# Causal convolution and two-layer MLP on one core: taps' diagonals from a bf16 table, a first convolution in 21 places, the first half of w_in in two pieces around x

## The chip, the cores and the metric

The kernel runs on one NeuronCore of a Trainium2 chip. A core has TensorE (matrix products into PSUM), VectorE, ScalarE and GpSimd (elementwise work; GpSimd also issues loads), SyncE (issues transfers) and they share 16 DMA engines. Each engine works through its own instructions in order; they wait for each other through semaphores. The metric is the device time of one execution in microseconds. Before the change it is 681.5 us, the median of 4 runs from 681.38 to 681.66.

## The reference

x has shape [8, 4096, 192], weight [8, 7], w_in [192, 2048], w_out [2048, 192], all in float32.

```python
w = softmax(weight)                       # over the 7 taps of each of 8 heads
y[b, s, c] = sum_k w[c // 24, k] * x[b, s + k - 6, c]     # zero before the start
h = y @ w_in                              # [32768, 2048]
out = maximum(0.01 * h, h) @ w_out        # [32768, 192]
```

The two products make up nearly all of the arithmetic; the convolution is a sum of seven shifted and scaled copies of x.

## The kernel before

**Layout.** Two batch rows are worked on together. The 192 channels are three chunks of 64; partitions 0 to 63 hold a chunk of the one row, 64 to 127 the same chunk of the other. xt is x in this layout (channels on partitions, time along the free dimension), yt the convolved x, g the activated first layer. A block is 512 time steps of a pair of rows; there are 32. The first two blocks are each done as two halves of 256 columns (groups 0 to 3), the others whole (groups 4 to 33).

**The main loop.** For each group, `mm1` forms the first layer in steps: step u makes 512 columns' worth of PSUM for both rows (`ph`, two buffers), in products of one 64-channel chunk with 128 columns of w_in (L494). ScalarE applies the leaky ReLU from PSUM into g (L501). Between the steps stand slots of the second layer for the group before (L511 for the first groups, L574 later). Meanwhile VectorE convolves the next group, tap by tap (L226, L232), GpSimd loads x three blocks ahead (L99), and SyncE transposes it by DMA (L117) and stores the results. The order on each engine is written out by hand; a plan tells how many second-layer slots follow each step.

**The beginning.** Group 0 has nothing ahead of it, so its convolution is done by TensorE. The softmaxed taps are split into bf16 parts (high, middle, low). `select` spreads them over the partitions by a product with a 0/1 matrix `sel`; VectorE copies the high and middle parts from PSUM to `whm` in float32 (L407). A diagonal of 64x64 for each tap, chunk and part is the 64-wide identity `ident2` times the tap: VectorE makes seven at once (`diag_wide`, L413), ScalarE makes some singly (`diag_each`, L421). `pe_conv_jobs` returns a list of jobs for one chunk: for each part and tap, two products of a 64x64 diagonal with the shifted xt, one per row (L257). TensorE works in four tiles of 64x64, so two chunks can run side by side if one of them writes crosswise (`cross=True`: row 0 to partitions 64 to 127 and the other way round); `apart` gives its two rows a PSUM buffer each. `run` interleaves lists. In group 0 the order is: chunk 0's first part alone; its second part beside chunk 2's first; chunk 1's one part beside chunk 2's second; chunk 1's other part alone. `evac` scales by 1/sum (`rsum`) and writes yt (L271, L276 on VectorE, L452 on ScalarE).

Behind it, TensorE transposes the next quarter of x (`transpose_first(1)`, from `x_rows`, L188), VectorE copies it to xt (`evac_first`, L199), and `mm1` of group 0 begins. Group 1's convolution is split: chunk 1 by VectorE, chunks 0 and 2 by TensorE in cuts between the first-layer steps of group 0 (`CUTS`: after steps 1, 3 and 5). The transposes of the third quarter stand after step 6, their copies at the end of the group.

**w_in.** It is loaded by GpSimd in two halves (`load_w_in`, L314), rows 0 to 127 and 128 to 191 each. Both tile rows need all chunks on their own partitions, so VectorE copies chunks across: `spread_down` (L320) and `spread_up` (L323). The order of loads on GpSimd's queue is: w_in's first half, x_rows 1, w_in's second half, x_rows 2, w_out in two, x_half 3 in six, then x_bf for block 2 on. VectorE spreads the second half between taps of group 1.

**Buffers.** `psum_o` (tag po) has four banks in turn, for the transposes, the convolution's sums and the second layer; `psum_h` (tag ph) two buffers of two banks, first used by the warm-up products (`warm`) and by `wps`, the selected taps.

## Time and profile before

| what | value |
|---|---|
| median of 4 runs | 681.5 us |
| the profiled execution | 681.55 us |
| its span, first to last instruction | 679.8 us |
| TensorE products, busy | 675.6 us, 99% |
| VectorE, busy | 481.2 us, 71% |
| ScalarE, busy | 518.7 us, 76% |
| granted TensorE clock, mean | 1.00 |
| first matmul of the first layer | 9.58 us |
| first matmul of the second layer | 17.83 us |

The span is what the trace covers; 1.75 us of the execution lie around it. A row of the timeline or of a group of instructions names the line, the engine, the operation, output<-input with their shapes, and how often it stands there; times are in us from the span's start, the mean of one instruction in ns. In brackets stands how long the engine was idle before it, and what ended that. The chain of waits is followed back from the last instruction: at each step to what released it. [...]

### The profile page before, as it was taken

Reading aid. Unit: us, or ns where it says so; the run is one execution under the profiler, and the core shown is the slowest. Engines: PE = TensorE matmul, PEld = TensorE weight load, DVE = VectorE, ACT = ScalarE, POOL = GpSimd, SP = SyncE. Lnnn points to the kernel's source line nnn. Section 1 sums busy time; section 2 is a strip of 40 time slices with the busy share of each in tenths; the row PEclk is TensorE's granted clock in tenths of the full one; section 3 lists DMA queues with packets and bytes.
Section 4 is the critical chain, followed back from the end, with each engine's and each line's share of the span. In section 5 each row is a group of like instructions: output and inputs, shape, how many; then the busy total and the mean of one; then the engine's idle time right before and its main releaser. Section 6 shows DMA issues by size and latency. Waiting matters only on the chain.

```text
span 679.8 us, 27093 instructions
## 1 busy us (share of the span) xinstructions
PE 675.6 (99%) x12444; PEld 446.9 (66%) x12444; DVE 481.2 (71%) x811; ACT 518.7 (76%) x608; POOL 146.3 (22%) x205
## 2 busy tenths in 40 slices
PE   9999999999999999999999999999999999999998
PEld 6997666666666666666666666666666666666667
DVE  7989468766768667778667687667786676876612
ACT  7899777777877778777777877777777777777781
POOL 7455220222210222211222012222022220000000
PEclk9999999999999999999999999999999999999999
DMA  9998864666556557456556475566465573321123
GB/s 152 92 114 106 59 87 80 80 62 75 88 85 89 69 56 90 81 87 87 61 68 89 79 95 71 59 85 93 74 87 67 62 96 71 72 56 32 35 49 94
DMA packets 213890, 53.27 MB, mean 78 GB/s; under 512 B 209296, under 2 KB 213392, under 8 KB 213776
## 3 DMA queue, kind: packets, MB, share of 16 engines
q0 software_dynamic: 98752, 13.97, 30.2%
q1 hardware_dynamic: 115008, 37.57, 28.0%
q8 instruction: 97, 1.59, 1.0%
q14 instruction: 17, 0.14, 0.1%
q10 hardware_dynamic: 16, 0.00, 0.0%
HBM read 28.31 MB, written 25.17 MB: 79 GB/s over the span
## 4 chain that ended last, share of the span: by engine, by line
PE 98%; DMA 1%; POOL 0%; issue 0%; DVE 0%; POOLq 0%
PE ph L494 49%; PE acc L574 44%; PE po L511 5%; DMA x_rows<-in_x_dram 1%; PE acc L257 0%; POOL w_in L314 0%; PE ptr L188 0%; POOL x_rows L148 0%; POOL sel L300 0%; DVE o_sb L624 0%; POOL ident masks.py:199 0%; POOL sel L298 0%; POOL ident masks.py:197 0%; POOLq masks.py:199 0%; POOLq L736 0%
## 5 line engine op out<-in xcount | busy, mean ns | idle before, releaser
L501 ACT ACTIVATE g<-ph 128x1024 bf16<-128x1024 f32 x512 | 496.6, 1021 | 140.8 <-PE ph L494 140.6
L232 DVE SCALAR_TENSOR_TENSOR yt<-xt,wk,yt 128x512 bf16<-128x512 bf16 (+1 forms) x582 | 381.6, 730 | 0.2
L494 PE MATMUL ph<-yt,w_in 64*64 64x512 bf16 (+2 forms) x6048 | 377.1, 369 | 0.0
L574 PE MATMUL acc<-g,w_out 64*64 64x512 bf16 x5568 | 339.9, 376 | 0.0
L494 PEld LDWEIGHTS <-w_in 64*64 64x64 bf16 (+1 forms) x6048 | 229.3, 131 | 103.0 <-issue 0.8
L574 PEld LDWEIGHTS <-w_out 64*64 64x64 bf16 x5568 | 178.4, 118 | 118.8
L99 POOL DMA_DIRECT2D x_bf<-in_x_dram x180 | 133.9, 773 | 409.6 <-DMA xt<-x_bf 407.5
L596 DVE STREAM_TRANSPOSE o_t<-acc 128x512 f32<-128x512 f32 x87 | 73.3, 884 | 181.7 <-PE acc L574 181.7
L511 PE MATMUL po<-w_out,g 64*128 64x192 bf16 (+1 forms) x640 | 36.8, 243 | 0.0
L511 PEld LDWEIGHTS <-g 64*128 64x128 bf16 (+1 forms) x640 | 32.6, 95 | 3.2 <-issue 0.4
L226 DVE TENSOR_SCALAR yt<-xt,wk 128x512 bf16<-128x512 bf16 (+1 forms) x97 | 29.7, 335 | 2.9 <-DMA xt<-x_bf 2.8
L584 ACT COPY junk<-junk 128x1 f32<-128x1 f32 x58 | 11.1, 192 | 4.1
L624 DVE COPY o_sb<-po 128x192 f32<-128x192 f32 x8 | 2.8, 356 | 6.8 <-PE po L511 4.1
L257 PE MATMUL acc<-xt,diag 64*64 64x256 bf16 x140 | 5.5, 272 | 0.2 <-ACT xt L199 0.2
L624 ACT COPY o_sb<-po 128x192 f32<-128x192 f32 x16 | 5.1, 323 | 0.3
L257 PEld LDWEIGHTS <-diag 64*64 64x64 bf16 x140 | 4.3, 106 | 1.3 <-issue 0.6
L358 PE MATMUL warm<-const-bfloat16-1.0 128*128 128x512 bf16 (+3 forms) x12 | 3.9, 478 | 0.8 <-PEq L736 0.8
L152 POOL DMA_DIRECT2D x_half<-in_x_dram x6 | 4.2, 718 | 0.8 <-DMA w_in<-in_moe_w_in_dram 0.8
L358 PEld LDWEIGHTS <-const-bfloat16-1.0 128*128 128x128 bf16 x12 | 1.4, 132 | 2.5 <-issue 2.5
L148 POOL DMA_DIRECT2D x_rows<-in_x_dram x4 | 2.9, 742 | 0.0
L413 DVE TENSOR_TENSOR diag<-ident,whm 128x448 bf16<-128x448 bf16 (+1 forms) x5 | 2.6, 580 | 0.0
L421 ACT ACTIVATE diag<-ident,whm 128x64 bf16<-128x64 bf16 x10 | 2.5, 338 | 0.0
(47 smaller groups left out, 23.7 us busy)
## 6 DMA issues: line engine op xcount, KB each, us to landing
out_dram<-o_t SPq DMA_DIRECT2D x112, 192.0 KB, 4.6
x_bf<-in_x_dram POOLq DMA_DIRECT2D x180, 64.0 KB, 3.3
out_dram<-o_sb SPq DMA_DIRECT2D x8, 192.0 KB, 3.2
xt<-x_bf SPq DMA_TRANSPOSE x90, 3.8
w_out<-in_moe_w_out_dram POOLq DMA_DIRECT2D x2, 384.0 KB, 7.8
out_dram<-o_t SPq DMA_DIRECT2D x8, 96.0 KB, 2.2
out_dram<-o_sb SPq DMA_DIRECT2D x8, 96.0 KB, 1.7
w_in<-in_moe_w_in_dram POOLq DMA_DIRECT2D x2, 256.0 KB, 5.4
```

Source lines behind the costliest of these rows:

```text
L99: ins = nc.gpsimd.dma_start(out=t[:, c, :, e, :], in_=src[2 * rp + e, :, :, c * CH : (c + 1) * CH],)
L226: lambda s=src, d=dst, c=c: nc.vector.tensor_scalar_mul(d, s, wk[:, c, 0:1])
L232: lambda s=src, d=dst, c=c, k=k: nc.vector.scalar_tensor_tensor(out=d, in0=s, scalar=wk[:, c, k : k + 1], in1=d, op0=mybir.AluOpType.mult, ...
L257: lambda k=k, p=p, a=a, ps=ps, to=to, acc=accs[e * apart]: nc.tensor.matmul(out=acc[to, :T], lhsT=diag[c][ps, p, k, :], rhs=xt[0][ps, c, a ...
L358: nc.tensor.matmul(out=wa[:, 0, 0:cols], lhsT=ones[:, 0:128], rhs=ones[:, 0:cols], start=True, stop=True,)
L494: nc.tensor.matmul(out=ph[m : m + M, e, i * T : (i + 1) * T], lhsT=w_in_of(f, e, c, m, m + M), rhs=y[ps, c, t0 : t0 + T], start=(c == chun ...
L501: act = nc.scalar.activation(out=g[blk][:, nf * u : nf * (u + 1), :, t0 : t0 + T], in_=ph.rearrange("p e (i t) -> p i e t", i=nf), func=my ...
L511: return nc.tensor.matmul(out=po[m], lhsT=g[b][ps, fc, e, s * 128 : (s + 1) * 128], rhs=w_out[ps, fc, :], start=start, stop=stop,)
L574: ins = nc.tensor.matmul(out=acc2[gi, r][e * CH : (e + 1) * CH, 0:T], lhsT=w_out_of(ps, fc, r), rhs=g[b][ps, fc, e, t0 : t0 + T], start=fi ...
L584: seal = nc.scalar.copy(out=junk, in_=junk)
L596: nc.vector.transpose(out=osb[gi, 0][:, 0 : T // GB, :, r], in_=acc2.pop((gi, r))[:, 0:T].rearrange("p (j k) -> p j k", k=GB),)
L624: ins = copy(out=o_sb[:, n % 2, :], in_=po.pop(n))
```

## The change

- `diag_wide` multiplies bf16 by bf16. The table `taps` holds each tap twice, side by side, in bf16, so that the innermost dimension of each operand is a pair of adjacent elements; it replaces `whm`. VectorE makes all six groups of seven diagonals, `diag_each` and ScalarE's ten are gone. The order on VectorE is new: chunk 0 and chunk 1 first, the small sums between, chunk 2 last.
- Group 0's convolution: chunks 0 and 1 run side by side in 14 places, then chunk 2 alone, in the new `pe_conv_quads`: each row's 256 columns are cut into two halves, one straight and one crosswise, so that all four tiles work, on 128 columns each. Its crosswise halves go to the two banks of `wps`. In all 14 places of 256 columns and 14 of 128, that is 21 places of 256 for the 28 before.
- One more warm-up product of 192 columns stands ahead of it.
- w_in comes in three pieces: 512, 512 and 1024 columns (`PIECES`). The first piece is loaded before x_rows 1, the second and the third after it. The spreads of the second and third stand between the first taps of group 1.
- The first step of group 0 runs over the chunks outermost (`wide`), so that chunk 1 and chunk 2 are needed later in it. The order of chunks is 0, 1, 2.
- wk is formed before the last evacuation of group 0 instead of after the copies of x.
- Group 1's cuts are 6, 6 and 2 jobs instead of 6, 5 and 3; chunk 2 of it has its rows in two buffers (`apart`) and its second row is evacuated by ScalarE. The transposes of the third quarter and their copies now stand after step 5, ahead of the last cut.

```diff
--- before.py
+++ after.py
@@ -44,16 +44,13 @@
     NBLK = (B // 2) * NB
     NHALF = 2
     RUN = 4
-    NPEC = 3
     FILL = 48
-    VK = 4
-    FIRST = (0, 2, 1)
     SKEW = [(c, k) for k in range(2) for c in range(2)]
     pair = iter([(0, 2), (1, 2), (0, 3), (1, 3), (0, 4), (1, 4), (0, 5)])
     for k in range(K):
         SKEW += [(2, k), next(pair)]
     SKEW += [(1, 5), (0, 6), (1, 6)]
-    CUTS = {1: (0, 6), 3: (6, 11), 5: (11, 14)}
+    CUTS = {1: (0, 6), 3: (6, 12), 5: (12, 14)}
     GB = 32
     NR = D // (2 * GB)
 
@@ -277,6 +274,42 @@
 
         return jobs, evac
 
+    def pe_conv_quads(grp, c, crossed):
+
+
+        blk, t0, T = grp
+        n = T // 2
+        acc = psum_o.tile([128, ST], FP32, name="acc", tag="po")
+        accs = [(acc, acc), (crossed[:, 0], crossed[:, 1])]
+        jobs = []
+        for p in range(2):
+            for k in range(K):
+                a = BASE + k + blk * ST + t0
+                four = []
+                for h in range(2):
+                    for e in range(2):
+                        ps = slice(e * CH, (e + 1) * CH)
+                        to = slice((e ^ h) * CH, ((e ^ h) + 1) * CH)
+                        four.append(
+                            lambda k=k, p=p, a=a + h * n, ps=ps, to=to, acc=accs[h][e]: nc.tensor.matmul(
+                                out=acc[to, :n], lhsT=diag[c][ps, p, k, :],
+                                rhs=xt[0][ps, c, a : a + n],
+                                start=(k == 0 and p == 0),
+                                stop=(k == K - 1 and p == 1),
+                            )
+                        )
+                jobs.append(four)
+
+        def evac(straight, *scale):
+            y = yt[blk][:, c, t0 : t0 + T]
+            straight(y[:, 0:n], acc[:, :n], rsum[:, c, :])
+            for e in range(2):
+                ps = slice(e * CH, (e + 1) * CH)
+                frm = slice((1 - e) * CH, (2 - e) * CH)
+                scale[e](y[ps, n:T], crossed[frm, e, :n], rsum[frm, c, :])
+
+        return jobs, evac
+
     def run(*lists):
         for slots in zip_longest(*lists, fillvalue=()):
             for both in slots:
@@ -305,15 +338,18 @@
     nc.vector.tensor_copy(out=sel[:, :, 1, :], in_=sel[:, :, 0, :])
 
 
-    NPW = 2
-    WF = F // NPW
-    w_in = [const_pool.tile([128, NCH, WF], BF16, name=f"w_in{n}") for n in range(NPW)]
+    PIECES = [(0, RUN), (RUN, 2 * RUN), (2 * RUN, NFC)]
+    w_in = [
+        const_pool.tile([128, NCH, (b - a) * 128], BF16, name=f"w_in{n}")
+        for n, (a, b) in enumerate(PIECES)
+    ]
 
     def load_w_in(n, rows):
         ps, slot = ((0, 128), 0) if rows == 0 else ((0, CH), 2)
+        a, b = PIECES[n]
         nc.gpsimd.dma_start(
             out=w_in[n][ps[0] : ps[1], slot],
-            in_=moe_w_in[rows : rows + ps[1], n * WF : (n + 1) * WF],
+            in_=moe_w_in[rows : rows + ps[1], a * 128 : b * 128],
         )
 
     def spread_down(n):
@@ -323,7 +359,8 @@
         nc.vector.tensor_copy(out=w_in[n][CH:128, 1:3, :], in_=w_in[n][0:CH, 0:3:2, :])
 
     def w_in_of(f, e, c, m0, m1):
-        n, f = divmod(f, NFC // NPW)
+        n = min(f // RUN, len(PIECES) - 1)
+        f -= PIECES[n][0]
         slot = c if c == 2 else c ^ e
         a = f // RUN * RUN * 128 + f % RUN
         return w_in[n][
@@ -335,8 +372,9 @@
     make_identity(nc, ident)
     load_w_in(0, 128)
     load_first(1)
-    for rows in (0, 128):
-        load_w_in(1, rows)
+    for n in range(1, len(PIECES)):
+        for rows in (0, 128):
+            load_w_in(n, rows)
     load_first(2)
 
 
@@ -403,48 +441,45 @@
     cast_first(0, 0, nc.scalar.copy)
     cast_first(0, 1, nc.scalar.copy, slice(0, 1))
     cast_first(0, 1, nc.vector.tensor_copy, slice(1, 2))
-    whm = const_pool.tile([128, NCH, 2, K + 1], FP32, name="whm")
-    nc.vector.tensor_copy(out=whm, in_=wps_hm)
-
-
-    diag = [const_pool.tile([128, 2, K, CH], BF16, name=f"diag{c}") for c in range(NPEC)]
-
-    def diag_wide(c, p, n):
+    taps = const_pool.tile([128, NCH, 2, K + 1, 2], BF16, name="taps")
+    nc.vector.tensor_copy(
+        out=taps, in_=wps_hm[..., None].to_broadcast([128, NCH, 2, K + 1, 2])
+    )
+
+
+    diag = [const_pool.tile([128, 2, K, CH], BF16, name=f"diag{c}") for c in range(NCH)]
+
+    def diag_wide(c, p):
+
+
+        shape = [128, K, CH // 2, 2]
         nc.vector.tensor_mul(
-            diag[c][:, p, 0:n],
-            ident2[:, None, :].to_broadcast([128, n, CH]),
-            whm[:, c, p, 0:n, None].to_broadcast([128, n, CH]),
-        )
-
-    def diag_each(c, p, ks):
-        for k in ks:
-            nc.scalar.activation(
-                out=diag[c][:, p, k, :], in_=ident2,
-                func=mybir.ActivationFunctionType.Copy, scale=whm[:, c, p, k : k + 1],
-            )
-
+            diag[c][:, p].rearrange("p k (m t) -> p k m t", t=2),
+            ident2.rearrange("p (m t) -> p m t", t=2)[:, None].to_broadcast(shape),
+            taps[:, c, p, 0:K, None, :].to_broadcast(shape),
+        )
 
     warm(1, 192)
     transpose_first(0, lambda: select(wps_l, slice(2, 3)))
     wps_l = wps_l[:, :, 0, 0]
     warm(1, ST)
     warm(1, 384)
+    warm(1, 192)
     evac_first(0, nc.scalar.copy, nc.scalar.copy)
-    for p in range(2):
-        diag_wide(0, p, K)
-    diag_wide(2, 0, K)
-    diag_wide(1, 1, VK)
-    diag_wide(2, 1, K)
-    diag_each(1, 1, range(VK, K))
-    diag_each(1, 0, range(K))
     wml = const_pool.tile([128, NCH, K + 1], FP32, name="wml")
-    nc.vector.tensor_add(wml, wps_l, whm[:, :, 1])
     rsum = const_pool.tile([128, NCH, 1], FP32)
+    diag_wide(0, 0)
+    diag_wide(1, 0)
+    diag_wide(0, 1)
+    nc.vector.tensor_add(wml, wps_l, taps[:, :, 1, :, 0])
+    diag_wide(1, 1)
     nc.vector.scalar_tensor_tensor(
-        out=rsum, in0=wml[:, :, K:], scalar=1e-9, in1=whm[:, :, 0, K:],
+        out=rsum, in0=wml[:, :, K:], scalar=1e-9, in1=taps[:, :, 0, K:, 0],
         op0=mybir.AluOpType.add, op1=mybir.AluOpType.add,
     )
+    diag_wide(2, 0)
     nc.vector.reciprocal(rsum, rsum)
+    diag_wide(2, 1)
     spread_down(0)
     spread_up(0)
 
@@ -454,20 +489,18 @@
         )
 
     pe_0, evac_0 = pe_conv_jobs(groups[0], 0)
-    pe_2, evac_2 = pe_conv_jobs(groups[0], 2, cross=True, apart=True)
-    pe_1, evac_1 = pe_conv_jobs(groups[0], 1, (1, 0))
-    run(pe_0[:K])
-    run(pe_0[K:], pe_2[:K])
+    pe_1, evac_1 = pe_conv_jobs(groups[0], 1, cross=True, apart=True)
+    pe_2, evac_2 = pe_conv_quads(groups[0], 2, wps)
+    run(pe_0, pe_1)
     evac_0(act_scale)
-    run(pe_1[:K], pe_2[K:])
-    run(pe_1[K:])
-    evac_2(act_scale, nc.vector.tensor_scalar_mul)
-    evac_1(act_scale)
+    evac_1(nc.vector.tensor_scalar_mul, act_scale)
+    wk = const_pool.tile([128, NCH, K], FP32, name="wk")
+    nc.vector.tensor_add(wk, taps[:, :, 0, 0:K, 0], wml[:, :, 0:K])
+    nc.vector.tensor_mul(wk, wk, rsum.to_broadcast([128, NCH, K]))
+    run(pe_2)
+    evac_2(nc.vector.tensor_scalar_mul, act_scale, act_scale)
     transpose_first(1)
     evac_first(1, nc.vector.tensor_copy, nc.vector.tensor_copy)
-    wk = const_pool.tile([128, NCH, K], FP32, name="wk")
-    nc.vector.tensor_add(wk, whm[:, :, 0, 0:K], wml[:, :, 0:K])
-    nc.vector.tensor_mul(wk, wk, rsum.to_broadcast([128, NCH, K]))
 
 
     g, po, acc2, osb, seal = {}, {}, {}, {}, None
@@ -484,9 +517,14 @@
         y = yt[blk]
         nf = ST // T
         ph = psum_h.tile([128, 2, ST], FP32, name="ph", tag="ph")
-        chunks = range(NCH) if blk or t0 else FIRST
-        for n in range(nf * NCH):
-            i, c = n // NCH, chunks[n % NCH]
+        chunks = range(NCH)
+
+
+        wide = not (blk or t0 or u)
+        order = [(i, c) for i in range(nf) for c in chunks]
+        if wide:
+            order = [(i, c) for c in chunks for i in range(nf)]
+        for i, c in order:
             f = nf * u + i
             for e in range(2):
                 ps = slice(e * CH, (e + 1) * CH)
@@ -495,8 +533,9 @@
                         out=ph[m : m + M, e, i * T : (i + 1) * T],
                         lhsT=w_in_of(f, e, c, m, m + M),
                         rhs=y[ps, c, t0 : t0 + T],
-                        start=(c == chunks[0]),
+                        start=(c == chunks[0] and not (wide and i)),
                         stop=(c == chunks[-1]),
+                        skip_group_check=wide,
                     )
         act = nc.scalar.activation(
             out=g[blk][:, nf * u : nf * (u + 1), :, t0 : t0 + T],
@@ -672,22 +711,24 @@
                 mm1(grp, u, 128 if i <= NSW else CH)
                 if i == 0 and u == 0:
                     conv_1 = conv_jobs(groups[1], (1,))
-                    for job in conv_1[:3]:
-                        job()
-                    spread_down(1)
-                    spread_up(1)
-                    for job in conv_1[3:]:
+                    for n in range(1, len(PIECES)):
+                        conv_1.pop(0)()
+                        spread_down(n)
+                        conv_1.pop(0)()
+                        spread_up(n)
+                    for job in conv_1:
                         job()
                     pe_0, evac_0 = pe_conv_jobs(groups[1], 0)
-                    pe_2, evac_2 = pe_conv_jobs(groups[1], 2, cross=True)
+                    pe_2, evac_2 = pe_conv_jobs(groups[1], 2, cross=True, apart=True)
+                if i == 0 and u == 5:
+                    transpose_first(2)
+                    evac_first(2, nc.vector.tensor_copy, nc.vector.tensor_copy)
                 if i == 0 and u in CUTS:
                     cut = slice(*CUTS[u])
                     run(pe_0[cut], pe_2[cut])
                 if i == 0 and u == 5:
                     evac_0(nc.vector.tensor_scalar_mul)
-                    evac_2(nc.vector.tensor_scalar_mul, nc.vector.tensor_scalar_mul)
-                if i == 0 and u == 6:
-                    transpose_first(2)
+                    evac_2(nc.vector.tensor_scalar_mul, act_scale)
             jobs = ahead[per * j : per * (j + 1)]
             if T == ST:
 
@@ -697,8 +738,6 @@
                     job()
                 jobs = []
             mm2_slots(i, quota[j] - sum(early))
-            if i == 0 and j == 3:
-                evac_first(2, nc.vector.tensor_copy, nc.vector.tensor_copy)
             if i == 1 and j == 1:
                 load_x(3, transpose_x(2))
             for job in jobs:
```

## The prediction

> **What bounds the kernel now.** I read the page first, then the chain of waits, then the chain and the timeline of the first 22 us, where the whole change lies. The page:
>
> ```profile
> PE 675.6 (99%) x12444; PEld 446.9 (66%) x12444; DVE 481.2 (71%) x811; ACT 518.7 (76%) x608; POOL 146.3 (22%) x205
> PE 98%; DMA 1%; POOL 0%; issue 0%; DVE 0%; POOLq 0%
> ```
>
> TensorE is the bound: 99% busy, 98% of the chain. What is won before its steady work starts moves everything after it; nothing else can be won. The chain in order of time (start, length, what):
>
> ```profile
> 4.31 4.77 DMA x_rows<-in_x_dram
> ...
> 9.13 0.52 PE ptr L188 x11
> 9.65 1.43 PE ph L494 x24
> 11.08 0.78 PE acc L257 x24
> ...
> 15.53 0.46 PE acc L257 x12
> 15.98 0.78 PE ph L494 x12
> 16.76 0.46 PE ptr L188 x12
> 17.22 0.78 PE ph L494 x12
> 18.00 0.25 PE po L511 x6
> ```
>
> The first layer waits for the second x_rows load, landed at 9.08; from 9.13 on TensorE hardly stops. The timeline (start, span, engine, instructions, idle before):
>
> ```profile
> 4.44 2.57 DVE L413 TENSOR_TENSOR diag<-ident,whm 128x448 bf16<-128x448 bf16 x5
> 5.33 3.35 PE L257 MATMUL acc<-xt,diag 64*64 64x256 bf16 x84 [0.19 <-ACT xt L199]
> 9.69 0.62 DVE L199 COPY xt<-ptr 128x384 bf16<-128x384 bf16 x2 [0.51 <-PE ptr L188]
> 12.08 0.42 DVE L320 COPY w_in<-w_in 64x1024 bf16<-64x1024 bf16 x1
> 12.54 0.69 DVE L323 COPY w_in<-w_in 64x2048 bf16<-64x2048 bf16 x1
> 14.80 3.03 ACT L501 ACTIVATE g<-ph 128x1024 bf16<-128x1024 f32 x3 [0.17 <-PE ph L494]
> ```
>
> The first conv runs 5.33 to 8.68. It ends 0.45 before x_rows is there, so a shorter conv alone would win nothing.
>
> [...] 448 elements with an fp32 table take 618 ns, 256 take 418, thus 1.04 ns per element and 151 fixed. [...] four 64*64 matmuls start within 0.02 us, one such step per 0.11 us, and each change of shape costs about 0.09. [...]
>
> **The change, part by part.** One profiled execution: 681.55 us, span 679.8, 1.75 around it; the median is 681.5.
>
> *Diagonals.* Table copy of 96 instead of 48 elements: 0.20 to 0.25. Six products of 448 elements[...]: half of 467 ns, plus the fixed 151, is 384 ns each. Starts today lie 0.54 apart (467 + 70, as the next one overlaps the end of the last), so then 0.30. The small ops between (wml, rsum, reciprocal) fill 0.1 each. They start at 4.49, 4.79, 5.10, 5.49, 5.87, 6.26; the last ends at 6.65. The conv can start at 5.33 as now (it waits for ScalarE's xt; the extra warm-up matmul ends before). It needs the second pair of products at 6.10 (ready 5.88), the last two at 6.87 and 7.25 (6.26, 6.65). ScalarE's ten diagonals (2.5 us) go; they were hidden.
>
> *First conv.* Today: 28 steps x 0.11 = 3.1 us. Then: 14 full steps of four 256-column matmuls, 1.54, and 14 of 128 columns. The nearest row for these is L188, pairs of 128 columns with 64-column weights: 0.056 per pair. Bounds: 0.056 (14 x 0.056 = 0.78) and 0.11 (no gain from narrow columns, 1.54). I take 0.056. Last start 7.59.
>
> *x_rows.* Ahead of it stand 384 KB of w_in now, 192 KB then (counted as written, in bf16). The landings today are w_in0 6.6 and 8.1, x_rows 8.6 and 9.1, w_in1 11.0 and 11.6: the 704 KB after the first took 5.0 us, 140 KB/us. 192 KB less is 1.4 us, so about 7.7. The other limit is the issue: 4.31 plus the 3.3 us that x_bf takes when the queues are free is 7.6[...]. Transposes are due at 7.59 + 0.15 = 7.74. I count no wait; each 0.1 later costs 0.1.
>
> *First layer.* Transposes 0.30, change 0.15: it starts at 8.19 (9.58 now). Its new order needs chunk 1 at 8.43, chunk 2 at 8.65. The last full conv step starts at 6.76 and ends 0.27 later. Chunks 0 and 1 then leave by rows L452 and L276 (0.47 each): ScalarE 7.07 to 7.55 and 7.45 to 7.91, VectorE 7.33 to 7.80. VectorE comes there from the spreads of w_in0: a copy takes 0.42 for 1024 elements and 0.69 for 2048, thus 0.29 for 512, and the two at half size end at 7.30. Chunk 2: VectorE after the two wk instructions, 7.97 to 8.32 (0.35 for 128 columns: 0.48 less 0.13); ScalarE twice 0.37 from 7.85, done 8.48. Ready with 0.15 to spare. So far **-1.39**.
>
> *VectorE's next chain.* Two x copies from 8.33 (after the transposes) to 8.95, scale 9.06 to 9.35, then spread, tap, spread, tap: 0.29, 0.49, 0.42, 0.49 with 0.03 between; w_in1 is spread at 10.64. TensorE wants it after two first-layer steps (9.58 to 11.01 today, 1.43) and six conv steps (11.01 to 11.80, 0.79), at 8.19 + 1.43 + 0.79 = 10.41: a new stall of **+0.27**. Then 0.42, 0.49, 0.69: w_in2 at 12.86; TensorE arrives at 10.68 + 1.43 + 0.79 = 12.90 (six conv steps in this cut, five now, 0.11). So the fifth first-layer step starts at 12.90 against 13.91: **-1.01**. The loads: w_in2 is whole after the same 960 KB as w_in1 today (11.0 and 11.6); wanted at 11.2 and 12.2. If the first is 0.2 late, so is all after.
>
> *Transposes of x_rows2 moved up.* One change of shape less (-0.09), a 0.08 wait for ScalarE and one conv step (0.11) less, and x_rows2 landed at 13.0, before 14.3. But they stood between the group's seventh and eighth step. The next group's first step needs the buffer of the group's seventh step (there are two ph buffers): from that step's start it is, as today, 0.89 until its activation starts, 1.02 until it ends and 0.04 for the signal, thus 1.95. TensorE has 0.68 + 0.65 (two steps) + 0.25 (three second-layer slots) = 1.58 to do: stall **+0.37**. From the fifth step to the second group: 4.17 both times, so nothing is won. The added ScalarE evacuation (0.37 net) ends just when the seventh step is ready. Behind the stall stand only TensorE's own steps; w_out landed at 14.7 and 16.7, the second half is wanted at 18.8.
>
> *GpSimd's queue.* Two more issues of about 0.58: x_rows2, w_out and the first x_half issues come 1.1 later, but still well ahead of their data (w_out issued 7.5, landed 14.7). The later issues wait for landings that do not move. SP's transposes of x_half start at 17.13, after that landing; the group that reads the last at 27.1 would read it at 25.2 and it lands at 25.1: covered, with nothing to spare, but that conv has 4 us before TensorE needs it.
>
> *After.* VectorE is full from 18 to 46 us (28.16 of 28.2), but reaches group 2's conv some 2 us earlier, TensorE 1.0. From 65 on TensorE alone decides. Sum: -1.39 + 0.27 + 0.11 = **-1.01**; 681.55 - 1.0 = **680.5**.
>
> **The rivals.** *Narrow steps at 0.11.* Eight instructions per 56 ns is twice the densest the trace shows (four in L188)[...]. All shifts by 0.76: 681.3. For 0.056: the second set of loads follows the first after 0.03.
> *Single-rate products.* If the engine doesn't double over the broadcast pair, six products at 0.54 end at 8.0. Conv starts at 5.69 and stalls 0.4 in it, VectorE's spreads and evacuations follow, w_in2 is spread at 14.3, and the fifth step is 0.45 later than now: 682.0, slower. It decides from 0.46 us between products on. Against it: the 64-element add.
> *Loads late.* w_in in 1024-byte rows and two more completions could push x_rows past 7.74 or w_in2 past 11.2; with 0.5 late, 681.0.
> *No stalls.* If VectorE's chain runs 0.3 quicker than I sum: 680.2.
>
> **How the numbers follow.** Mine 0.64 (680.3 to 680.8), narrow steps in full or part 0.14, single rate 0.08, late loads 0.09, no stalls 0.05. The range, 680.1 to 681.5, leaves out single rate and the tails. 0.2% is 1.36 us, about what a measurement of this kernel can tell from no change; only a gain with no stall at all, or single rate with a further wait, passes it: faster 0.08, same 0.87, slower 0.05.
>
> **What would show it.** Products 0.38 us long; L254 and L294 together ending near 7.8; the first layer at 8.2 without a wait on x_rows; two TensorE gaps, about 0.3 before the third first-layer step (on L359) and 0.4 before the second group (on ScalarE). The prediction is wrong if the narrow steps lie 0.11 apart, products last 0.6, or x_rows lands after 7.8.

## The result

The kernel after takes 682.44 us (median of 41 runs, 681.47 to 683.23), the kernel before, measured beside it, 681.42 (61 runs, 681.05 to 682.54): a ratio of 1.0014, interval 1.0009 to 1.0018. So it is 1.0 us slower where 1.0 us faster was predicted, outside the range of 680.1 to 681.5; in size it lies within the 0.2% that the prediction calls about what a measurement can tell from no change, though the interval leaves out 1. The profiled execution of after took 682.56 us, its span is 680.9.

The page of the kernel after, busy time by engine and the chain of waits by engine:

```profile
PE 676.1 (99%) x12473; PEld 443.6 (65%) x12473; DVE 481.1 (71%) x814; ACT 517.0 (76%) x600; POOL 147.6 (22%) x207
PE 98%; DVE 1%; ACT 1%; issue 0%; DVEq 0%
```

TensorE's share is what it was. What changed is the remaining 2%: DMA is gone from the chain, VectorE and ScalarE have come in. The chain of after in order of time (start, length, what) says where:

```profile
5.87 0.18 DVE wml L474
...
7.44 0.75 DVE w_in L359
...
9.18 0.35 DVE yt L305
9.53 0.54 DVE xt L196 x2
...
10.17 0.65 DVE yt L223
...
11.69 0.43 DVE w_in L359
12.12 0.05 issue
12.17 1.50 PE ph L532 x23
13.66 0.78 PE acc L254 x24
14.45 1.03 PE ph L532 x12
15.48 0.02 issue
15.50 1.94 ACT g L540 x2
17.44 0.03 issue
17.47 0.47 ACT yt L487
17.93 0.02 issue
17.96 1.03 ACT g L540
18.99 0.04 issue
19.03 0.85 PE ph L532 x12
```

Before, the chain came from x_rows' landing into TensorE at 9.13 and stayed there. Now VectorE's queue holds it without a break from 5.87 to 12.12, and ScalarE's from 15.50 to 18.99. The timeline of TensorE (start, span, instructions, idle before and its releaser) shows the same as gaps. The first layer's rows of before at the four places of the table below, none with a wait in front of it:

```profile
9.58 1.50 PE L494 MATMUL ph<-yt,w_in 64*128 64x256 bf16 x24
11.80 1.51 PE L494 MATMUL ph<-yt,w_in 64*128 64x256 bf16 x24
13.91 1.61 PE L494 MATMUL ph<-yt,w_in 64*128 64x256 bf16 x24
18.08 0.82 PE L494 MATMUL ph<-yt,w_in 64*128 64x256 bf16 x12
```

In the kernel after:

```profile
8.47 0.53 PE L185 MATMUL ptr<-ident,x_rows 128*64 128x128 bf16 x12
8.93 1.82 PE L532 MATMUL ph<-yt,w_in 64*128 64x256 bf16 x24
12.17 1.50 PE L532 MATMUL ph<-yt,w_in 64*128 64x256 bf16 x23 [0.41 <-DVE w_in L359]
14.38 1.74 PE L532 MATMUL ph<-yt,w_in 64*128 64x256 bf16 x24
19.03 0.85 PE L532 MATMUL ph<-yt,w_in 64*128 64x256 bf16 x12 [0.43 <-ACT g L540]
```

A step has 12 products, so a row of 24 is two steps. (Each of these products is recorded with 0.27 to 0.30 us, and 24 of them stand in a row of 1.50: their records overlap.) The four places to compare throughout are these:

| start, us | before | predicted | after |
|---|---|---|---|
| first layer | 9.58 | 8.19 | 8.93 |
| its third step | 11.80 | 10.68 | 12.17 |
| its fifth step | 13.91 | 12.90 | 14.38 |
| second group | 18.08 | 17.07 | 19.03 |

The first layer did start 0.65 earlier. At the third step the lead is gone (one product began at 11.46; the table takes the 23 of that row that waited), and the second group starts 0.95 late, nearly the whole 1.01 between the two profiled executions. From there on nothing is regained.

### The profile page after: what moved, and what is told of

Same layout as the page of the kernel before. It is cut to its first block, busy times and chain, and to the rows that moved or that the text cites. A ratio compares the mean times of both kernels' runs of the same rounds, so it can differ in the third digit from the quotient of the medians.

```text
span 680.9 us, 27150 instructions
## 1 busy us (share of the span) xinstructions
PE 676.1 (99%) x12473; PEld 443.6 (65%) x12473; DVE 481.1 (71%) x814; ACT 517.0 (76%) x600; POOL 147.6 (22%) x207
## 4 chain that ended last, share of the span: by engine, by line
PE 98%; DVE 1%; ACT 1%; issue 0%; DVEq 0%
PE ph L532 48%; PE acc L613 44%; PE po L550 5%; PE warm L396 1%; ACT g L540 0%; DVE w_in L359 0%; DVE diag L456 0%; PE acc L254 0%; DVE yt L223 0%; PE ptr L176 0%; DVE w_in L356 0%; DVE xt L196 0%; DVE yt L273 0%; DVE yt L229 0%; ACT yt L487 0%
## 5 line engine op out<-in xcount | busy, mean ns | idle before, releaser
L613 PEld LDWEIGHTS <-w_out 64*64 64x64 bf16 x5568 | 175.7, 118 | 121.5
L550 PEld LDWEIGHTS <-g 64*128 64x128 bf16 (+1 forms) x640 | 34.2, 95 | 2.2 <-issue 0.4
L254 PE MATMUL acc<-xt,diag 64*64 64x256 bf16 x112 | 4.1, 285 | 0.0
L254 PEld LDWEIGHTS <-diag 64*64 64x64 bf16 x112 | 2.9, 113 | 1.0 <-DVE diag L456 0.5
L350 POOL DMA_DIRECT2D w_in<-in_moe_w_in_dram x6 | 3.4, 594 | 0.0
L487 ACT ACTIVATE yt<-acc,rsum 64x256 bf16<-64x256 f32 (+1 forms) x3 | 1.4, 469 | 2.4 <-PE acc L254 2.4
```

What stands on the lines that cost most here:

```text
L254: lambda k=k, p=p, a=a, ps=ps, to=to, acc=accs[e * apart]: nc.tensor.matmul(out=acc[to, :T], lhsT=diag[c][ps, p, k, :], rhs=xt[0][ps, c, a ...
L550: return nc.tensor.matmul(out=po[m], lhsT=g[b][ps, fc, e, s * 128 : (s + 1) * 128], rhs=w_out[ps, fc, :], start=start, stop=stop,)
L613: ins = nc.tensor.matmul(out=acc2[gi, r][e * CH : (e + 1) * CH, 0:T], lhsT=w_out_of(ps, fc, r), rhs=g[b][ps, fc, e, t0 : t0 + T], start=fi ...
```

## Experiments

All times are medians, each ratio against the kernel before on the same chip. "Whole" is the time of the last of the 16 landings that the trace records for a load's second part.

### Is it the clock, or the phase of the start?

In the profile of after the TensorE clock is granted at 6.35 us, in that of before at 4.03; as long as it is missing products are slower (three transposes take 0.49 us from 4.43 on, in before 0.33 from 4.44 on), and the first conv starts at 5.76 instead of 5.33 for it. Two kernels hold all work back behind 14 memsets on VectorE, with warm-up products meanwhile:

```diff
+    hold = const_pool.tile([128, ST], FP32, name="hold")
+    warm(18, ST)
+    for _ in range(14):
+        held = nc.vector.memset(hold, 0.0)
-    warm(6, ST)
+    warm(11, ST)      # the first of them, and each queue's first load, wait for held
```

Before, held:

> The kernel before, with every queue's first work held behind 14 fills of a 512-column tile on VectorE (about 7.7 us) while TensorE multiplies ones, so that the clock is granted before the real work begins. Clock theory (the changed kernel loses because TensorE's full clock came at 6.2 us in its profile and at 4.0 in that of before): this is before plus the hold, about 689.1, since before has its wait for x_rows to cover a late clock anyway. Rival (the clock has no part): the same 689.1. It is the base for hold_after.

After, held:

> The same hold in front of the changed kernel. Clock theory: with the clock granted ahead the difference to hold_before falls from +1.0 us to between -1.0 and 0 (the sum of the prediction, less what VectorE's copies lose behind GpSimd's issues). Rival, VectorE's chain alone (the two pieces of w_in between taps, stretched copies): the difference stays near +1.0.

Measured: 691.45 (4 runs, ratio 1.0143, 1.0129 to 1.0157) and 692.01 (4 runs, 1.0147, 1.0131 to 1.0162). The hold shifts the work by 9.3 us (VectorE's copy of `sel` begins at 11.23 instead of 1.95), not by the 7.7 assumed, so the expected 689.1 was missed. With the clock on in both convs the first layer starts 1.03 earlier in after than in before (18.46 against 19.49). The total is 0.56 higher by the medians of four runs each, with intervals that overlap almost wholly: neither the -1.0 to 0 of the clock theory nor clearly the +1.0 of its rival. So an early clock did not bring the gain back here, but what share of the 1.0 us the late clock has is not settled by this pair. (The profile of after held is of the slowest of its four runs, 694.82; TensorE stood idle there for 1.33 us up to 23.16, and the clock was lower once more from 23.33 to 26.74: 24 conv products took 1.41 instead of 0.85. Nothing finer is read from it.) A further profile of the kernel before:

> The kernel before once more, for a second profile. Clock theory: whenever the full clock comes, up to about 6.5 us, the first matmul of the first layer stays near 9.6, as the load of x_rows (9.1) covers it, and the time is 681.1 to 681.8. Rival (a late clock costs before as much): with a clock later than in the first profile, the first layer starts later by the same.

It took 681.6 us, its clock came at 4.03 again. Whether before hides a late clock was not seen. One other execution bears on the clock: in the profile of the next kernel, a variant of after, it came at 3.58, earlier than in before, and that execution still took 682.01, against 681.55 of before.

### VectorE's queue: GpSimd's issues and the warm-up product

The chain through VectorE has copies that last longer than their like. VectorE's timeline, of the kernel before:

```profile
10.72 0.29 DVE L226 TENSOR_SCALAR yt<-xt,wk 128x256 bf16<-128x256 bf16 x1
```

and of the kernel after, then GpSimd's issues there:

```profile
7.44 0.75 DVE L359 COPY w_in<-w_in 64x1024 bf16<-64x1024 bf16 x1
10.17 0.65 DVE L223 TENSOR_SCALAR yt<-xt,wk 128x256 bf16<-128x256 bf16 x1
11.69 0.42 DVE L359 COPY w_in<-w_in 64x1024 bf16<-64x1024 bf16 x1
12.66 0.42 DVE L356 COPY w_in<-w_in 64x1024 bf16<-64x1024 bf16 x1
13.63 0.94 DVE L359 COPY w_in<-w_in 64x2048 bf16<-64x2048 bf16 x1
```

```profile
7.17 1.49 POOL L145 DMA_DIRECT2D x_rows<-in_x_dram  x2
9.97 1.50 POOL L149 DMA_DIRECT2D x_half<-in_x_dram  x2
```

The first and the third are copies of one shape, 0.75 and 0.42; the second took 0.29 in the kernel before, the last, by the prediction's line, 0.69. The long ones began 0.2 to 0.3 us after GpSimd had begun to issue a load (a further issue began at 13.38), and were stretched by 0.25 to 0.36 us. Not each copy under an issue was: in before one of 1024 elements began at 12.08, 0.12 after an issue, and took its 0.42. The expectations call the stretching the port theory; what holds such a copy up was not shown. The prediction had not counted it. One kernel moves GpSimd's later issues behind those copies, another drops the added warm-up product:

```diff
-    load_first(2)
-    (w_out's two loads, load_first(3), load_x(2))
-    spread_up(0)
+    load_first(2, spread_up(0))     # its issue waits for this copy
+    (w_out's wait for the first tap, load_first(3) for the last spread)
```

> The changed kernel with GpSimd's later loads held back: x_rows2 behind VectorE's spread of the first piece of w_in, w_out behind the first tap of group 1, x_half and x_bf behind the last spread. Port theory (copies that start 0.2 to 0.5 us after a load was issued wait 0.25 to 0.37 us): the spread of 64x1024 takes 0.42 instead of 0.75, the tap of 256 columns 0.29 instead of 0.65, the spread of 64x2048 0.69 instead of 0.94, and the time falls by about 0.7 to 681.7. Clock theory alone: the durations fall at most a little and the time stays at 682.4. If the later loads then become a bound, it is slower.

```diff
     warm(1, 384)
-    warm(1, 192)
```

> The kernel after without its added warm-up product of 192 columns. It ends ahead of the first conv's other wait when the clock is on by 4 us, and then its absence gives nothing: 682.3 to 682.6. Where the clock comes on past 5.5 us the product stands on the conv's path for up to 0.16 us, and since the fifth step waits for w_in's last piece, even that is lost: less than 0.1 us.

Measured: 682.23 (13 runs, 1.0012, 1.0004 to 1.0020) and 682.16 (21 runs, 1.0014, 1.0007 to 1.0020), neither to be told from after; the second is a little under its expectation. In the first the copies' durations came as the port theory had said, its time of 681.7 didn't. No copy is long any more and the clock came at 3.58: the first layer starts at 8.35, within 0.16 of the prediction. Yet its third and fifth steps still wait, and now for another reason: the spreads of w_in's second and third pieces stand waiting for the loads. VectorE's timeline of that run:

```profile
10.02 0.29 DVE L360 COPY w_in<-w_in 64x512 bf16<-64x512 bf16 x1 [0.25 <-DMA w_in<-in_moe_w_in_dram]
12.38 0.42 DVE L360 COPY w_in<-w_in 64x1024 bf16<-64x1024 bf16 x1 [0.59 <-DMA w_in<-in_moe_w_in_dram]
```

and a line of its chain:

```profile
6.12 6.24 DMA w_in<-in_moe_w_in_dram
```

The third step is at 11.33, the fifth at 14.10. Behind VectorE's delay stood w_in's late landing, of nearly the same size.

### w_in in pieces

Three kernels: before with the three pieces alone; after with two halves again; after with x_rows behind the second piece, its transposes behind the second step, and the third quarter's transposes back in their old place.

```diff
 before, pieces alone:
-    NPW = 2
+    PIECES = [(0, RUN), (RUN, 2 * RUN), (2 * RUN, NFC)]
 after, halves:
-    PIECES = [(0, RUN), (RUN, 2 * RUN), (2 * RUN, NFC)]
+    PIECES = [(0, 2 * RUN), (2 * RUN, NFC)]
 after, x_rows behind the second piece:
-    load_first(1)
     (load_w_in(1, ..))
+    load_first(1)
     (load_w_in(2, ..))
```

> The kernel before with w_in in three pieces alone, loaded and spread in the order of the kernel after. Theory A: the DMA engines are half idle from 8 to 9 us as in the kernel after, w_in's last piece lands at 11.9 and 13.1, the fifth step starts near 14.4 (13.9 before) and the time is 0.3 to 0.7 us above before's: 681.7 to 682.1. Theory B: the DMA engines stay over 0.9 busy, the last piece lands by 11.7, the fifth step starts at 13.9 or sooner and the time is 680.9 to 681.4.

> The kernel after with w_in in two halves as before (loads, spreads and their place among the taps as before); all else as after. Theory A (the cut is what costs): the last half's pieces land at 11.0 and 11.6 as in the kernel before, the 16 DMA engines stay over 0.9 busy from 8 to 9 us, the first layer starts near 9.6 (x_rows lands at 9.1, as before), the fifth step near 13.9 and the second group near 18.1 to 18.5; 681.5 to 681.9. Theory B[...]: the DMA engines are half idle from 8 to 9 us here too, the second half lands past 12.3, the fifth step starts past 14.3 and the time is 682.3 or more.

> The kernel after with x_rows loaded behind w_in's second piece instead of ahead of it, its transposes behind the second step of the first layer instead of ahead of the first, the second piece's spread right behind the first's on VectorE, and the third block's transposes back between the seventh and eighth step. If the first layer is set by w_in's pieces and not by TensorE, the first step starts by 8.4 and the third without waiting, by 10.6; the fifth then waits for w_in's last piece. Theory A (the queue runs dry behind the small pieces): the last piece lands by 12.4 since x_rows fills the gap, the fifth step starts by 13.6 and the time is 681.0 to 681.4. Theory B: it lands past 13, the fifth step starts past 14.2 and the time is 681.7 to 682.2.

Measured: pieces alone 682.16 (21 runs, 1.0010, 1.0004 to 1.0017), halves 682.19 (13 runs, 1.0009, 1.0000 to 1.0017), x_rows later 682.44 (21 runs, 1.0014, 1.0008 to 1.0021). The pieces alone cost the kernel before 0.7 us. TensorE's timeline of that run:

```profile
9.10 1.50 PE L499 MATMUL ph<-yt,w_in 64*128 64x256 bf16 x24
12.15 1.50 PE L499 MATMUL ph<-yt,w_in 64*128 64x256 bf16 x23 [0.54 <-DVE w_in L326]
14.81 1.50 PE L499 MATMUL ph<-yt,w_in 64*128 64x256 bf16 x23 [0.26 <-DVE w_in L326]
```

The first layer starts 0.48 earlier than before (x_rows comes sooner, as meant), and the fifth step 0.9 later. So the loss comes with the cut, as theory A had it. Theory B, that VectorE's faster products keep GpSimd's loads back, falls: the old products (0.62 us in the trace of before, 0.38 in that of after) are in this kernel. A's details were not all met: the engines were 0.89 busy from 8 to 9 us, though at 88 GB/s, the last piece came at 12.36 and 14.05, later than 11.9 and 13.1, and with it the fifth step at 14.81 instead of 14.4. With halves, in turn, w_in was whole at 12.46 and not 11.6 as A expected, the fifth step came at 14.38, not 13.9, without a wait for it (x_rows landed at 9.10, the first two steps waited 0.2 for VectorE's part of the last chunk, and the second cut has a conv step more), and the rest was lost to ScalarE, below; its time is above A's 681.5 to 681.9 and just under B's 682.3, though the engines were 1.16 busy from 8 to 9 us and not half idle, as B had it. In the third kernel the last piece still came at 13.00, though x_rows stood where the queues had run dry; TensorE waited 0.43 for ScalarE and 0.72 for VectorE's copies of x instead, and its expectations of 681.0 to 681.4 and of 681.7 to 682.2 both failed.

How dry the queues run shows in the stretches of the profile (window, TensorE, its loads, VectorE, ScalarE, GpSimd, clock, share of the 16 DMA engines, GB/s). Before:

```profile
8.00:9.00 1.00, 0.87 (x17) 0.52 (x9) 0.90 (x2) 0.82 (x3) 0.91 (x2) 1.00 1.17 162
```

After:

```profile
8.00:9.00 1.00, 1.00 (x54) 0.82 (x44) 0.90 (x4) 0.95 (x3) 1.00 (x2) 1.00 0.45 69
```

With the same bytes ahead, the engines move 69 GB/s where they moved 162, since what came first is done and w_in's last piece has hardly begun. (The share in this view can pass 1, as the 1.17 of before does.) The packets in the two traces say the same: of the 192 packets of 2048 bytes that make up the last half, 64 began in this microsecond in before and 22 in after, though there too GpSimd's issues of them had ended, at 7.24.

### Why the last piece is late

The landings of w_in's last half in the profiles: with two halves, four loads ahead of it, whole at 11.56, 11.93, 11.27, 12.46, 11.70, 11.73, 11.02 and once 13.10; with pieces, six loads ahead, at 13.09, 12.99, 14.05, 13.88, 13.29, 13.03, 13.00. All six loads of w_in in after, with the times of their issues and the time from issue to landing:

```profile
L350 POOL DMA_DIRECT2D w_in<-in_moe_w_in_dram x6: 537/588/679, 1.9 to 6.7; - x6
DMA to landing us min/median/max: 3.2/4.2/6.4
```

The last is the slowest: issued at 6.66, whole 6.4 us later. Against before three things differ: GpSimd issues the last half 1.1 us later (at 6.1 and 6.7), the rows ahead are 1024 bytes long instead of 2048, and two more loads stand ahead. Three kernels take them apart: a GpSimd memset ahead of the issues, in before and in after, and in before the first half in four loads by rows, of 2048 bytes each.

```diff
 before, issue later:
+    nc.gpsimd.memset(idle, 0.0)          # 128 x 1920 bf16
     for rows in (0, 128):
         load_w_in(1, rows)
 after, issue later: the same ahead of load_w_in(2, ..)
 before, four loads by rows:
-    load_w_in(0, 0)
-    load_w_in(0, 128)
+    load_part(0, CH), load_part(CH, CH)
+    load_part(128, CH // 2), load_part(128 + CH // 2, CH // 2)
```

> The kernel before with one GpSimd memset of about 1.1 us ahead of the issues of w_in's second half; pieces, bytes and order unchanged. Theory I (the landing follows the issue): issues at 6.1 and 6.7 instead of 5.0 and 5.6, the half is whole at 12.6 to 13.0 instead of 11.3 to 11.7, its spread ends 14.0 to 14.4, the fifth step starts 14.2 to 14.6 instead of 13.9 and the time is 681.7 to 682.1. Theory Q (the small pieces slow the queues; with whole halves the queue has work enough until 9 us): whole by 11.8, fifth step 13.9, 681.3 to 681.6.

> The kernel after with the same memset between the issues of w_in's second and third piece. Theory I: the third piece, whole at 13.0 to 13.3 after issues at 6.1 and 6.7, comes 1.1 later, at 14.1 to 14.4; the fifth step starts near 15.6 and the time is 683.2 to 683.7. Theory Q: the queues are behind by more than 1 us already, so it lands by 13.6 and the time is within 0.4 us of after's, 682.2 to 682.8.

> The kernel before with each of the two loads of w_in's first half cut in two by rows: four loads instead of two, rows of 2048 bytes as before, the same bytes in the same order. Theory N (the number of loads ahead, each with its issue of 0.57 us, is what makes the last half late): the last half lands past 12.9, as in all runs with pieces by columns, the fifth step starts past 14.2 and the time is 681.8 to 682.3. Theory R (the 1024-byte rows, twice as many packets for the same bytes, are what does it): it lands by 12.2, within the spread of the runs with whole halves, 681.3 to 681.7.

Measured: 683.94 (6 runs, 1.0035, 1.0023 to 1.0048), 683.01 (10 runs, 1.0022, 1.0013 to 1.0032), 682.28 (13 runs, 1.0011, 1.0003 to 1.0019). The two times with a memset say nothing on w_in, since in both an instruction of VectorE was long as well (1.78 and 1.32 us, below). Their landings do. In before, issued at 6.66 and after, the half was whole at 11.21, no later than without; in after, issued at 7.76 and after, at 13.02, again no later. So it isn't the issue time by itself, theory I. Four loads by rows: whole at 13.81, in VectorE's and TensorE's timelines of that run

```profile
13.57 0.42 DVE L320 COPY w_in<-w_in 64x1024 bf16<-64x1024 bf16 x1 [1.47 <-DMA w_in<-in_moe_w_in_dram]
14.77 1.50 PE L502 MATMUL ph<-yt,w_in 64*128 64x256 bf16 x23 [0.51 <-DVE w_in L323]
```

The time and the landing are those that theory N named, and row length by itself, theory R, isn't needed for the lateness. By medians the half is whole at 11.70 with four loads ahead (nine profiles) and at 13.06 with six in pieces (eight), 1.4 us apart. But that the number of loads is the cause is not shown, only that it goes with the lateness. The packets say that it need not be one lateness: half of the 192 had begun by 9.2 in before, by 9.5 with four loads by rows, and only by 10.3 in after. In after the whole half comes later; with four loads by rows only its last packets do (until 13.3), and the second try below, with four loads ahead and its 13.10, has such a tail too. The loads by rows also reach 64 and 32 partitions each, where the halves reach 128 and 64, and no kernel separates that from their number. There is one profile for each kernel.

### ScalarE ahead of the second group

Three kernels: after with the third quarter's transposes back behind the seventh step; after with the second group's last evacuation back on VectorE; before with that evacuation on ScalarE and nothing else.

```diff
 after, transposes back:
-                if i == 0 and u == 5:
+                if i == 0 and u == 6:
                     transpose_first(2)
 after, evacuation back:
-                    evac_2(nc.vector.tensor_scalar_mul, act_scale)
+                    evac_2(nc.vector.tensor_scalar_mul, nc.vector.tensor_scalar_mul)
 before, evacuation on ScalarE: the same line the other way round
```

> The kernel after with the third block's transposes back between the seventh and the eighth step. If ScalarE's 0.43 us of waiting before the second group's first evacuation comes from moving them, it goes, and the time falls by 0.3 to 0.45 us to 682.0 to 682.1. The rival, that the second group is set by what the first group left late on TensorE, gives the same time as after within 0.15 us (682.3 to 682.6), with the wait on another engine.

> The kernel after with one word changed: the second half of the second group's crossed evacuation, given to ScalarE by the change, is back on VectorE. Theory S: from the fifth first-layer step to the second group ScalarE is the bound (three activations of 1.0 us and 0.9 before the first), and 0.47 us put among them costs 0.47 less what TensorE would have waited anyway; the second group comes 0.25 to 0.45 us earlier after the fifth step and the time is 682.0 to 682.2. The rival, that the transposes' new place costs it, keeps the time at 682.3 to 682.6.

> The kernel before with that one evacuation on ScalarE and nothing else. Theory S: 0.3 to 0.45 us slower, 681.8 to 682.0, with TensorE waiting for ScalarE ahead of the second group (18.08 becomes 18.4 to 18.5). The rival, that ScalarE has room here: 681.4 to 681.6, second group at 18.1.

Measured: 682.17 (19 runs, 1.0012, 1.0005 to 1.0019), 681.99 (21 runs, 1.0007, 1.0001 to 1.0014), 681.87 (13 runs, 1.0009, 1.0000 to 1.0017). The last changes one operand and is 0.45 us slower than before by the medians (the interval just reaches 1); the second changes the same operand the other way and is 0.45 us below after. TensorE's and ScalarE's timelines of the last:

```profile
13.61 1.61 PE L494 MATMUL ph<-yt,w_in 64*128 64x256 bf16 x24
18.32 0.85 PE L494 MATMUL ph<-yt,w_in 64*128 64x256 bf16 x12 [0.38 <-ACT g L501]
14.49 1.94 ACT L501 ACTIVATE g<-ph 128x1024 bf16<-128x1024 f32 x2 [0.17 <-PE ph L494]
16.75 0.47 ACT L452 ACTIVATE yt<-acc,rsum 64x256 bf16<-64x256 f32 x1 [0.32 <-DVE yt L276]
17.24 4.05 ACT L501 ACTIVATE g<-ph 128x1024 bf16<-128x1024 f32 x4
```

From the fifth step to the second group it takes 4.71 here, in before 4.17. ScalarE's own work was 3.96 of those (0.89 to the first activation, three of 1.0, the signal), so 0.2 were free, and an evacuation of 0.47 doesn't fit. The 4.71 holds 0.32 more, in which ScalarE waited for VectorE's evacuation of the other row: in before both rows share a PSUM buffer, in after they don't, and no such wait is there. Without it 4.39 are left. In after it is 4.65, of which 0.24 is a wait inside the step for VectorE's last spread of w_in (1.74 us for two steps that take 1.50 elsewhere), so 4.41; with the evacuation back it is 4.2. The transposes' place makes no difference that can be told: with them back the wait goes but ScalarE's chain is as long, the profile shows 4.4, and the time lies between the two ranges that were expected.

### What the conv alone gives, and three tries to make it count

The first conv and its diagonals alone, all else as before; then the second block's transposes behind the second step and w_in's upper spread in two column halves; the transposes behind the first step; and last the second column half behind the second step in the program.

```diff
 conv alone = after, halves + transposes back + evacuation back
 first try:
-    spread_up(0)
+    spread_up(0, slice(0, RUN * 128))      # and the other half behind the conv
-    transpose_first(1)
+                if i == 0 and u == 1:
+                    transpose_first(1)
 second try: the transposes at u == 0, the other half right behind their copies
 third try: the other half at u == 1
```

> The change's diagonals and its conv of the first group alone: w_in in two halves, the third block's transposes and the second group's evacuation as before. The conv ends by 8.4 but x_rows lands at 9.1 as before, so the first layer starts at 9.6 and the gain in the conv is hidden; the first layer's new order waits some 0.2 us for VectorE's part of the last chunk. Second group 18.2 to 18.4, 681.5 to 681.8. If the conv or its products cost more than that elsewhere: 682.0 or more.

> The same with the second block's transposes moved from ahead of the first layer to behind its second step, so that the first layer doesn't wait for x_rows, and the upper spread of w_in's first half in two column halves, the second behind VectorE's part of the conv. If w_in's first half (landed near 8.0, spread near 8.6) sets the first layer: first step 8.7 to 9.0, fifth 13.1 to 13.4, second group 17.3 to 17.6, 680.7 to 681.0. The rival: the transposes' copies on VectorE come 0.5 us later and TensorE waits for them at the first conv cut (by 0.7 us in the earlier run with the transposes in this place), so that the fifth step is at 13.8 and the time within 0.15 us of before.

> The diagonals and the conv of the change with w_in in two halves, the second group's evacuation and the third block's transposes as before, the second block's transposes behind the first step of the first layer, and the upper spread of w_in's first half in two column halves, the second behind those transposes' copies. The first step at 8.6 to 8.9, the transposes at 9.3 to 9.6, the cut behind the second step without a wait for xt, the fifth step at 13.4 to 13.7: 681.0 to 681.3. The rival, that what is won at the first step is lost to VectorE's later copies and spreads, gives a fifth step past 13.9 and 681.5 to 682.0.

> As the run before with the second block's transposes behind the first step, but with the second column half of the spread behind the second step in the program, so that this step doesn't wait for it. First step 7.8 to 8.6, second without a wait on w_in, third by 11.3, fifth at 13.3 to 13.8 (set by w_in's second half), second group 17.5 to 18.0: 680.9 to 681.3, faster than before by 0.1 to 0.5. The rival: w_in's second half lands past 12.3 as in the run before and takes the gain back: 681.5 to 682.0.

Measured: 681.88 (13 runs, 1.0004, 0.9996 to 1.0012), 682.83 (11 runs, 1.0022, 1.0013 to 1.0031), 682.33 (21 runs, 1.0013, 1.0007 to 1.0020), 681.62 (13 runs, 1.0000, 0.9992 to 1.0009). The conv alone, just above what was expected, is not to be told from before: it ends by 8.6, and x_rows lands at 9.12. The tries start the first layer early and lose it again: in the first, waits of 0.67 for the spread and 0.72 for the copies of x; in the second 0.73 for the spread, and w_in's second half whole only at 13.10; in the third nothing but 0.29 at the first step, but its first layer, at 9.29 with a conv that began at 5.76, came too late to show a gain (that profile is of the slowest of its runs, 682.25). The first two missed all that was expected of them. The time of the third lies in its rival's range, but not for the rival's reason, since w_in was whole at 11.02. None of the kernels beats before.

## Why the prediction was wrong

- **Diagonals: right.** Products of 364 to 393 ns, with 384 predicted. That the 1.04 ns per element would halve was the author's estimate; in the trace of before one row alone speaks for it, the 64-element bf16 add of L383: 173 ns, where 151 + 64 x 1.04 gives 218. Over the pairs in `taps` it did: with the same fixed part, (384 - 151) / 448 = 0.52 ns per element. The rival with the single rate falls.
- **Conv: right.** The places of 128 columns lie 0.056 apart, and their weight loads kept to that, 56 within 0.90 us. The start was 0.43 late where the clock came late.
- **x_rows: right.** Landed at 7.35, no wait for it; the first layer at 8.35 in the run without stretched copies and with the clock at 3.58, 8.19 predicted.
- **VectorE's next chain: the step that failed first.** The prediction has w_in1 spread at 10.64; it was spread at 12.12, 1.48 late. The terms: 0.42 waiting for the warm-up product under the late clock; 0.33 and 0.36 for two stretched instructions that began under GpSimd's issues, counted at nothing; 0.26 because the two wk instructions take 0.43, not 0.17, and had taken as long in the trace of before; the remaining 0.1 in gaps. The claim that chunk 2 is ready with 0.15 to spare fell with it: the first two steps took 1.82 instead of 1.50, waiting for VectorE's part of it. In the profiled execution this chain set what followed too: the fifth step came behind the third with no further wait, the last piece's first spread began at 12.66, right behind a tap and with no wait for the load, and the 0.24 lost inside the fifth step was for the spread at 13.63, one of the long copies.
- **"w_in2 is whole after the same 960 KB as w_in1 today": the step that failed behind it.** It was whole at 11.9 and 13.1, not 11.0 and 11.6, and at 12.4 and 13.0 in the run without stretched copies; there the spreads wait for the loads, 0.25 and 0.59. When the second piece is wanted and lands was not worked out at all. Taking VectorE's delays away moved the fifth step only from 14.38 to 14.10; 12.90 was predicted. The pieces alone, in the kernel before, cost 0.7 us. The bytes were the wrong measure: behind the same bytes the last half came 1.4 us later by the medians. "Loads late" stood among the rivals with 0.5 us and 0.09; the direction was there, its size was not. The prediction followed up what GpSimd's two more issues do to all that comes after w_in, but not to w_in's own last piece.
- **Transposes and the added evacuation: stall right in size, balance wrong.** A stall of 0.37 was predicted and 0.43 seen, on ScalarE, at the second group. The 0.28 that TensorE saves in that stretch was set against it and called even; that leaves 0.09 by the prediction's own numbers. And it could not count, because ScalarE's queue sets the stretch. The added evacuation was to end just when the seventh step is ready: it ended at 17.93, the step was ready 0.2 earlier, at 17.74. So the stretch took 4.41 without the wait for w_in instead of 4.17, +0.24.
- **The sum.** 1.48 at the fifth step and 0.48 from there to the second group (the 0.24 of waiting for the last spread and this 0.24) make 1.96, and 680.55 + 1.96 = 682.5; the profiled execution took 682.56. Of the rivals none is met as it was written: the slow side came from transfers and two in-order queues, not from the products.

What isn't settled: why w_in's last half comes later behind more loads, and how much of the difference the late clock makes in those executions that have it.

## What to carry to other kernels

A gain at the head of a pipeline counts only up to the next thing that lands or drains at its own time: list for each later wait what else would hold it there, and expect the second one to stand right behind the first (here VectorE's queue at 12.1, w_in at 13.1, ScalarE from 15.5). Don't count a load's landing by the bytes ahead of it alone: here cutting a load to get its first part sooner went with 1.4 us more for the last part. An instruction moved to an idle engine is free only if that engine is idle in that stretch; its mean load (76% here) doesn't tell.

## What the runs showed that was not expected

Two instructions of VectorE lasted 1.32 and 1.78 us while GpSimd was at work. In the kernel after with the later issue, a copy of 512 elements, 0.29 us elsewhere, began 0.56 us after the memset and ended 0.14 us after it. GpSimd's and VectorE's rows:

```profile
6.12 1.74 POOL L378 MEMSET idle<- 128x1920 bf16 x1
6.68 1.32 DVE L356 COPY w_in<-w_in 64x512 bf16<-64x512 bf16 x1
```

In before with the later issue a cast of 8 elements, 0.16 us in the other profiles, lasted from 3.25 to 5.03 while GpSimd issued loads, and the first conv came 1.8 us late for it; why this cast was long, and the same cast in the other kernels not, is open. The TensorE clock was granted between 3.58 and 6.41 us after the start in the profiles that record it, for programs that begin alike; in before with the later issue, where the first conv was late too, it came at 9.19.
